# Scores and PV of an attention kernel in one place on TensorE from unit 14 on, with half of PV in two banks of the matmul pool

## Chip, cores and metric

One core of a Trainium2 chip. The metric is the time of one execution in microseconds of device time, given as a median over runs. "Span" is the time from the first to the last instruction in the trace; it is some 1.7 us shorter than the run's time.

## The reference

Attention within chunks of 64 rows, followed by a two-layer network whose activation is h * sigmoid(beta * h).

```python
# attention: q, k, v of 8 batches x 8 heads x 576 rows x 64
scores = scale * np.matmul(q_c, k_c.transpose(0, 1, 2, 4, 3))   # within chunks of 64
attn = np.exp(scores - max) / sum
out = np.matmul(attn, v_c)                                        # "PV"
# network: x of 4608 x 512, w_in 512 x 2048, w_out 2048 x 512
h = x @ w_in
g = h * (1.0 / (1.0 + np.exp(-beta * h)))
result = g @ w_out
```

## The kernel before

The 4608 rows are worked off in 18 units of 256, two units to a block, so 9 blocks. While a block's network runs (16 tiles `hps` of x @ w_in, called m0 to m15 here, and four result tiles `ops` of g @ w_out for the block before), the attention of the next block's two units is slipped in between. `tanh` on ScalarE (ACT) and one multiply on VectorE (DVE) turn an `hps` tile into g.

The accumulators take eight PSUM banks: four in the matmul pool, two for scores, two for PV.

```python
ps_p = ctx.enter_context(tc.tile_pool(name="ps_p", bufs=4, space=bass.MemoryType.PSUM))  # hps, ops
ps_s = ctx.enter_context(tc.tile_pool(name="ps_s", bufs=1, space=bass.MemoryType.PSUM))  # scores: 2 banks
ps_x = ctx.enter_context(tc.tile_pool(name="ps_x", bufs=1, space=bass.MemoryType.PSUM))  # PV: 2 banks
...
def emit_sc(u, split=False, later=False):
    qt, kt = qT.pop(u), kT.pop(u)
    sc = ps_s.tile([128, 2, H, CH], FP32, tag="s", name="sc")
    ...                                  # 32 matmuls of 64x64x64
    nc.scalar.activation(out=et, in_=sc, func=ACTF.Exp, scale=scale)
...
def emit_pv(u, where=("x", "s")):        # first half in the PV banks, second half in the score banks
    et = et_t.pop(u)
    for s in range(2):
        i = 2 * u + s
        if where[s] == "p":              # or in two banks of the matmul pool
            x = [ps_p.tile([128, 4, 128], FP32, tag="p", name=f"y{r}") for r in range(2)]
        else:
            pool = {"x": ps_x, "s": ps_s}[where[s]]
            x = [pool.tile([128, 2, 4, 128], FP32, tag=where[s], name="x")]
        ...                              # 16 matmuls of 64x64x65
...
def emit_norm(u, s):                     # DVE: reciprocal of the sums, multiply; this frees the banks
    ...
# a block: items with a position from 0 to 1, sorted, then emitted
for j in range(3, NB):
    items = [(0.02 + 0.98 * m / KFF, 0, ("m", m)) for m in range(KFF)]
    for t in range(4):
        for hf in range(2):
            items.append((0.98 * (t + 0.5 * hf) / 4, 1, ("t", t, hf)))
    if j + 1 < NB:
        for i in range(2):
            items += att_items(2 * j + 2 + i, 0.03 + 0.43 * i, 0.43)   # scores at 0.03, PV at 0.20, ...
```

So a unit interrupts the big matmuls (128 rows, 128 columns, 512 wide) in two places: once for its scores, once for PV. Each is a group of 32 small matmuls in 64x64 tiles of the array; I call such a group a visit.

The softmax here doesn't subtract the row's maximum and nothing guards it: scores larger than these inputs give would overflow.

## Time and profile before

| what | value | from |
|---|---|---|
| time, median of 3 | 288.98 us (288.93 to 289.1) | runs |
| span | 287.5 us | page |
| TensorE (PE) busy | 281.2 us, 98% | page |
| PE busy from 180 to 240 us | 60.00 of 60.00 | windows |
| DVE, ACT busy | 49%, 51% | page |
| cost of one visit of 32 small matmuls | 0.48 us, eight times in units 14 to 17 | starts of single matmuls |

PE is the bound, without a gap in the stretch that the change touches. How the cost of a visit is read is in the prediction.

### The profile page before, as it was taken

Reading aid. Unit: us, or ns where it says so; the run is one execution under the profiler, and the core shown is the slowest. Engines: PE = TensorE matmul, PEld = TensorE weight load, DVE = VectorE, ACT = ScalarE, POOL = GpSimd, SP = SyncE. Lnnn points to the kernel's source line nnn. Section 1 sums busy time; section 2 is a strip of 40 time slices with the busy share of each in tenths; the row PEclk is TensorE's granted clock in tenths of the full one; section 3 lists DMA queues with packets and bytes.
Section 4 is the critical chain, followed back from the end, with each engine's and each line's share of the span. In section 5 each row is a group of like instructions: output and inputs, shape, how many; then the busy total and the mean of one; then the engine's idle time right before and its main releaser. Section 6 shows DMA issues by size and latency. Waiting matters only on the chain.

```text
span 287.5 us, 6650 instructions
## 1 busy us (share of the span) xinstructions
PE 281.2 (98%) x2779; PEld 136.2 (47%) x2779; DVE 141.4 (49%) x253; ACT 146.7 (51%) x224; POOL 95.7 (33%) x125
## 2 busy tenths in 40 slices
PE   8889999999999999999999999999999999999995
PEld 4464456545544444444444444444444444444444
DVE  2678444776567554534454445444453536333300
ACT  4377218774557545454545454555445544444411
POOL 8743579397172992060907060000000000000000
PEclk9999999999999999999999999999999999999999
DMA  8999999999999999999999999614252212010012
GB/s 197 174 197 206 169 178 209 211 163 173 153 94 182 155 176 179 153 130 159 132 167 134 145 155 142 134 49 110 75 113 73 73 39 73 36 39 36 36 73 75
DMA packets 139997, 37.14 MB, mean 129 GB/s; under 512 B 126912, under 2 KB 135488, under 8 KB 139968
## 3 DMA queue, kind: packets, MB, share of 16 engines
q0 software_dynamic: 99136, 17.83, 79.7%
q1 hardware_dynamic: 40688, 18.83, 30.5%
q8 instruction: 22, 0.36, 0.5%
q14 instruction: 7, 0.06, 0.1%
q10 hardware_dynamic: 144, 0.07, 0.1%
HBM read 36.71 MB, written 9.44 MB: 161 GB/s over the span
## 4 chain that ended last, share of the span: by engine, by line
PE 94%; DMA 3%; ACT 1%; issue 1%; DVE 0%; POOL 0%; DVEq 0%; POOLq 0%
PE hps L322 44%; PE ops L354 42%; DMA h<-in_k_dram 3%; PE x L264 2%; PE sc L236 1%; PE sc L223 1%; PE ops L580 1%; ACT xt L297 1%; PE xp L296 1%; PE sc L196 0%; ACT et L206 0%; POOL h L394 0%; PE warm L374 0%; PE xp L304 0%; DVE xt L297 0%
## 5 line engine op out<-in xcount | busy, mean ns | idle before, releaser
L336 DVE SCALAR_TENSOR_TENSOR gt<-sg,hps 128x512 f16<-128x512 f32 (+1 forms) x153 | 99.1, 654 | 108.5 <-ACT sg L332 108.3
L332 ACT ACTIVATE sg<-hps,beta 128x512 f32<-128x512 f32 (+1 forms) x153 | 100.4, 663 | 74.0 <-PE hps L322 73.9
L322 PE MATMUL hps<-xt,win 128*128 128x512 f16 (+1 forms) x612 | 136.7, 367 | 0.8 <-ACT xt L297 0.7
L354 PE MATMUL ops<-wout,gt 128*128 128x512 f16 x560 | 131.3, 379 | 0.0
L322 PEld LDWEIGHTS <-win 128*128 128x128 f16 x612 | 58.0, 98 | 61.9 <-issue 1.0
L354 PEld LDWEIGHTS <-gt 128*128 128x128 f16 x560 | 53.7, 98 | 63.1
L364 ACT ACTIVATE osb<-ops 128x512 f32<-128x512 f32 x35 | 20.9, 598 | 42.2 <-PE ops L354 42.2
L112 POOL DMA_DIRECT2D vbig<-in_v_dram x40 | 34.0, 872 | 10.3 <-DMA wout<-in_moe_w_out_dram 3.7
L98 POOL DMA_DIRECT2D qu<-in_q_dram x22 | 18.7, 865 | 39.5 <-DMA qT<-qu 37.2
L280 DVE TENSOR_TENSOR x<-x,rd 128x512 f16<-128x512 f32 x34 | 23.5, 692 | 1.3
L98 POOL DMA_DIRECT2D ku<-in_k_dram x22 | 18.9, 880 | 0.1
L278 DVE RECIPROCAL rd<-x 128x8 f32<-128x8 f32 x34 | 6.8, 201 | 11.1 <-PE x L264 11.1
L245 ACT ACTIVATE et<-sc 128x1024 f16<-128x1024 f32 (+1 forms) x8 | 6.4, 811 | 8.2 <-PE sc L236 8.2
L229 ACT ACTIVATE et<-sc 128x1024 f16<-128x1024 f32 x10 | 10.1, 1015 | 0.0
L264 PEld LDWEIGHTS <-et 64*64 64x64 f16 x576 | 6.0, 107 | 7.3 <-issue 3.4
L374 PE MATMUL warm<-idle 128*128 128x512 f16 x24 | 8.6, 515 | 0.0
L264 PE MATMUL x<-vbig,et 64*64 64x65 f16 x544 | 7.8, 195 | 0.2 <-ACT et L206 0.2
L104 POOL DMA_DIRECT2D ku<-in_k_dram x9 | 6.8, 755 | 2.5 <-DMA win<-in_moe_w_in_dram 1.3
L104 POOL DMA_DIRECT2D qu<-in_q_dram x9 | 6.8, 767 | 1.9 <-DMA win<-in_moe_w_in_dram 1.1
L592 DVE TENSOR_SCALAR osb<-ops 128x256 f32<-128x256 f32 (+1 forms) x2 | 0.7, 358 | 12.1 <-PE ops L580 12.1
L130 POOL DMA_DIRECT2D win<-in_moe_w_in_dram x8 | 6.0, 751 | 1.2 <-DMA h<-in_k_dram 0.8
L177 DVE STREAM_TRANSPOSE t<-h 128x512 f32<-128x512 f32 x4 | 4.2, 1084 | 4.2 <-ACT h L176 3.7
(46 smaller groups left out, 69.3 us busy)
## 6 DMA issues: line engine op xcount, KB each, us to landing
out_dram<-osb SPq DMA_DIRECT2D x35, 256.0 KB, 3.4
vbig<-in_v_dram POOLq DMA_DIRECT2D x32, 128.0 KB, 7.6
qu<-in_q_dram POOLq DMA_DIRECT2D x20, 128.0 KB, 5.3
ku<-in_k_dram POOLq DMA_DIRECT2D x20, 128.0 KB, 6.6
win<-in_moe_w_in_dram POOLq DMA_DIRECT2D x8, 256.0 KB, 9.7
wout<-in_moe_w_out_dram POOLq DMA_DIRECT2D x4, 512.0 KB, 12.4
qu<-in_q_dram POOLq DMA_DIRECT2D x3, 256.0 KB, 7.3
ku<-in_k_dram POOLq DMA_DIRECT2D x3, 256.0 KB, 8.9
```

What stands on the lines that cost most here:

```text
L98: nc.gpsimd.dma_start(out=tv[off:off + n, sp], in_=src[b, :, s:s + n, :].rearrange("h p d -> p h d"),)
L104: nc.gpsimd.dma_start(out=t[off // 2:(off + n) // 2], in_=src[b, :, s:s + n, :].rearrange("h (p r) d -> p h r d", r=2),)
L112: nc.gpsimd.dma_start(out=vbig[off:off + n, i, :, 0:D], in_=v[b, :, s:s + n, :].rearrange("h p d -> p h d"),)
L229: nc.scalar.activation(out=et, in_=sc, func=ACTF.Exp, scale=scale)
L264: nc.tensor.matmul(out=(x[0][64 * c:64 * c + 64, r, g, 0:D + 1] if len(x) == 1 else x[r][64 * c:64 * c + 64, g, 0:D + 1]), lhsT=(et[64 * r ...
L280: nc.vector.tensor_tensor(out=o, in0=z[..., 0:D], in1=rd[:, r].to_broadcast(list(o.shape)), op=ALU.mult)
L322: nc.tensor.matmul(out=hps[:, 0:n], lhsT=w_in16[m // 2][:, kk, (m % 2) * 128:(m % 2) * 128 + 128], rhs=xr[:, c0 // CH:(c0 + n) // CH, 2 * ...
L332: nc.scalar.activation(out=sg[:, 0:n], in_=hps[:, 0:n], func=ACTF.Tanh, scale=beta2[:, m:m + 1])
L336: nc.vector.scalar_tensor_tensor(out=gt_t[j][:, m, c0:c0 + n], in0=sg[:, 0:n], scalar=1.0, in1=hps[:, 0:n], op0=ALU.add, op1=ALU.mult,)
L354: nc.tensor.matmul(out=ops, lhsT=gt_t[j][:, kk, t * 128:(t + 1) * 128], rhs=w_out16[kk // 4][:, kk % 4, :], start=(kk == 0), stop=(kk == K ...
L364: nc.scalar.activation(out=osb, in_=ops, func=ACTF.Copy, scale=0.5)
L374: nc.tensor.matmul(out=d[:, 0:w], lhsT=idle[:, 0:128], rhs=idle[:, 0:w])
```

## The change

Its intent: enter the small tiles less often. From unit 14 on, PV of a unit and the scores of the next stand in one place, so units 14 to 17 need five visits, not eight. For this, PV's second half may not lie in the score banks, since the next scores follow at once; it goes, first in order, into two of the four matmul-pool banks. The scores of unit 14 move ahead into block 5, and so do the transposes of unit 15.

```diff
+    MU = 14
@@ emit_pv
-        for s in range(2):
+        for s in (1, 0) if u >= MU else (0, 1):
@@
+    def emit_norms(u):
+        for s in (1, 0) if u >= MU else (0, 1):
+            emit_norm(u, s)
+            emit_xt_dma(u, s)
@@ the items of a block
-            if j + 1 < NB:
+            if 2 * j + 2 < MU:
                 for i in range(2):
                     items += att_items(2 * j + 2 + i, 0.03 + 0.43 * i, 0.43)
+                if 2 * j + 4 == MU:
+                    items += [(0.80, 2, ("sc", MU)), (0.82, 3, ("T", MU + 1))]
+            elif j + 1 < NB:
+                for i in range(2):
+                    items.append((0.15 + 0.5 * i, 2, ("hop", 2 * j + 2 + i)))
@@ emitting them
+                elif it[0] == "hop":
+                    emit_pv(it[1], ("x", "p"))
+                    if it[1] + 1 < NU:
+                        emit_sc(it[1] + 1)
+                    if it[1] + 2 < NU:
+                        emit_T(it[1] + 2)
+                    emit_norms(it[1])
```

In the list of items, `sc` are the scores of a unit, `T` the transposes of its q and k, `norm` the work of DVE that empties the PV banks, and `hop` a merged visit.

## The prediction

> **What bounds the kernel now.** I first read the page's busy times, the clock row and the chain that ended last.
>
> ```profile
> PE 281.2 (98%) x2779; PEld 136.2 (47%) x2779; DVE 141.4 (49%) x253; ACT 146.7 (51%) x224; POOL 95.7 (33%) x125
> PEclk9999999999999999999999999999999999999999
> PE 94%; DMA 3%; ACT 1%; issue 1%; DVE 0%; POOL 0%; DVEq 0%; POOLq 0%
> ```
>
> TensorE (PE) is busy for 98% of the span at full clock, and the chain is 94% PE. DVE and ACT are half idle. Busy can hide gaps, because matmuls overlap, so I asked for the stretch that the change touches:
>
> ```profile
> 180.00:240.00 60.00, 60.00 (x517) 27.45 (x516) 28.68 (x49) 30.91 (x46) 0.00 (x0) 1.00 0.34 81
> ```
>
> 60.00 of 60.00 us are busy on PE (columns: length, then PE, weight load, DVE, ACT, POOL). GpSimd issues nothing more there. So the only thing to gain is PE time spent badly, and any wait that reaches PE is paid in full. The PE timeline shows where time is spent badly:
>
> ```profile
> 196.76 1.89 PE L322 MATMUL hps<-xt,win 128*128 128x512 f16 x8
> 198.58 0.45 PE L223 MATMUL sc<-qT,kT 64*64 64x64 f16 x32
> 198.96 1.90 PE L354 MATMUL ops<-wout,gt 128*128 128x512 f16 x8
> 200.69 1.89 PE L322 MATMUL hps<-xt,win 128*128 128x512 f16 x8
> ```
>
> The columns are start, length, engine, line, and the group. I read starts, not lengths, since one matmul shows 379 ns but eight take 1.73 us, 216 ns each. From 196.76, eight matmuls end their turn at 198.49; scores start at 198.58, 0.09 late. The 32 small matmuls hold PE until 198.96, and the next eight take 1.73, of which the records of single instructions show 10 ns more than usual for the first. By those records a visit costs: entry 93 ns, first to last small start 252, last start to next large start 125, slow first large one 10; 480 together. All eight visits of units 14 to 17 (four of scores, four of PV) read 470 to 472 plus 10. Streaming needs 8 turns of 4 at 32 ns, 256; so some 220 ns of each visit are the price of going in and out. Is that price paid per visit, not per matmul? An earlier visit of 64 small ones answers:
>
> ```profile
> 80.22 2.54 PE L322 MATMUL hps<-xt,win 128*128 128x512 f16 x11
> 82.69 0.71 PE L236 MATMUL sc<-qT,kT 32*64 32x64 f16 x64
> 83.33 1.04 PE L322 MATMUL hps<-xt,win 128*128 128x512 f16 x4
> 84.20 1.89 PE L354 MATMUL ops<-wout,gt 128*128 128x512 f16 x8
> ```
>
> It starts at 82.69, 0.09 after 80.22 + 11 x 0.216, and lasts 0.64; with the 10 ns it costs 0.74 us, not 0.96. So it is paid per visit.
>
> **What the Trainium skill says.** "TensorEngine Tiling (Array Packing)", Key Properties: changing the tiling mode, not just the tile, drains TensorE. The trace agrees: 64*64 groups between 128*128 groups cost 93 ns on entry and a late exit. The change lives on this. "PSUM — Partial Sum Buffer", Terms: there are eight banks of 2 KiB per partition, and two engines may not be in one bank and quadrant at once. The kernel's pools take all eight (4 for the matmul pool, 2 for scores, 2 for PV), so PE must wait until DVE or ACT has finished reading a bank. The trace of before shows these waits as met in time, with no PE idle after 16 us.
>
> **The change part by part.** Per unit, before has two visits, scores and PV. After has, by the order of instructions in the built kernel: scores of 14 alone, earlier, late in block 5; then PV(14)+scores(15), PV(15)+scores(16), PV(16)+scores(17); then PV(17) alone. The matmuls are the same, 5560 PE rows in both. DVE gains 4 rows: each PV half in two banks is normalised in two pieces. These rows lie in idle DVE time, except where they delay a release.
>
> *Gain.* Eight visits become five. A merged visit is 0.74 us (the 64-matmul visit above) against 2 x 0.48 = 0.96: 0.22 saved, three times: **-0.66 us**.
>
> *Wait 1: scores of 14, moved into block 5.* They use the score banks, which still hold the second half of PV(13) there. In after they come behind the matmul tile m12 of block 5. Everything until then has the same order in both kernels, so before's trace gives the times:
>
> ```profile
> 176.80 1.89 PE L354 MATMUL ops<-wout,gt 128*128 128x512 f16 x8
> 176.86 0.69 DVE L336 SCALAR_TENSOR_TENSOR gt<-sg,hps 128x512 f16<-128x512 f32 x1 [2.38 <-ACT sg L332]
> ...
> 178.30 0.68 DVE L336 SCALAR_TENSOR_TENSOR gt<-sg,hps 128x512 f16<-128x512 f32 x1
> 178.53 1.89 PE L322 MATMUL hps<-xt,win 128*128 128x512 f16 x8
> 178.90 0.20 DVE L278 RECIPROCAL rd<-x 128x8 f32<-128x8 f32 x1
> 179.13 0.69 DVE L280 TENSOR_TENSOR x<-x,rd 128x512 f16<-128x512 f32 x1
> ```
>
> m12 is the first half of the group at 178.53. Its turn ends at 179.39, and scores would start at 179.48 with the entry. The multiply that empties PV(13)'s second half ends at 179.13 + 0.69 = 179.82. A release takes about 0.06 to reach PE: early in the kernel a copy ends at 14.98 + 0.58 = 15.56 and the matmul that waits for it starts at 15.62.
>
> ```profile
> 14.98 0.58 ACT L297 COPY xt<-xp 128x512 f16<-128x512 f16 x1 [0.36 <-PE xp L296]
> 15.62 0.27 PE L322 MATMUL hps<-xt,win 128*128 128x256 f16 x1 [0.67 <-ACT xt L297]
> ```
>
> So 179.88 against 179.48: **+0.40 us**, once.
>
> *Wait 2: the matmul pool during a merged visit.* PV's second half takes two of its four banks. In after each merged visit stands between two hps tiles, and the next ops tile follows; by the release order it gets the bank of the hps tile just before the visit. Call that tile's start 0. The chain is read in before's timeline:
>
> ```profile
> 200.69 1.89 PE L322 MATMUL hps<-xt,win 128*128 128x512 f16 x8
> 201.76 0.69 ACT L332 ACTIVATE sg<-hps,beta 128x512 f32<-128x512 f32 x1 [1.47 <-PE hps L322]
> 202.47 0.69 DVE L336 SCALAR_TENSOR_TENSOR gt<-sg,hps 128x512 f16<-128x512 f32 x1 [2.38 <-ACT sg L332]
> ```
>
> Tanh starts 1.07 after the tile, DVE 1.78, and DVE ends at 2.47; with 0.06, PE may write at 2.53. PE wants it after the tile (0.86), the merged visit (0.74) and one more tile (0.87): 2.47. **+0.06, three times: +0.18 us.** After PV(17) there are no scores, so PE wants it 0.26 earlier, at 2.21: **+0.32 us**.
>
> *What I checked and count as zero.* The tile right behind the visit uses the bank of an ops copy that ends at 0.85; it is wanted at 1.60. The PV banks themselves are emptied by about 3.0 and 3.6 (DVE free at 2.38; per bank a reciprocal of 0.17 and a multiply of 0.42, which overlap a little) and are wanted at 4.2 and 5.1. The exponential of the scores (1.0 us) ends at 2.7, when tanh of the next tile becomes ready. The transposed x of units 15 and 17 is issued behind the q and k transposes; in the quiet stretch those take 1.25 us each to issue and x 1.19, landing 2.4 later: about 212 us for unit 15, wanted at about 214.6. q and k of 15 are transposed about 2 us earlier now and land some 3 us before use.
>
> *Sum.* -0.66 + 0.40 + 0.18 + 0.32 = **+0.24 us**. 288.98 + 0.24 = **289.2 us**.
>
> **The rivals.** *A: the gain as intended, no waits*: 288.98 - 0.66 = 288.3. For it: DVE is half idle, and before shows no PE wait here. Against it: the waits before scores of 14 and after PV(17) have margins of -0.4 and -0.3 us by the records, not by guess. *B: the two banks lent to PV starve the matmuls badly*, because the norms stand in DVE's queue before the next tiles' work: each visit loses up to 1 us, so about 291 to 292. For it: two of four banks are gone for some 3 us. Against it: those banks are wanted over 1 us after they come free, and the copies and tanh in between have room. *C: the merge saves less*, since PV uses other rows, banks and weights than scores and the second group's waits for DMAs are queue instructions in the middle of 128 small ones: up to 0.3 us lost per visit. Then 289.5 to 289.8. The 64-matmul visit speaks against it, but it is all of one kind. *D: hidden anyway*: not on this engine, which has no slack.
>
> **Range and chances.** Gain and waits are each under 1 us, against 5.8 us that 2% would take. The gain is sure to about 0.2; the three waits of 0.06 could vanish or double; the three runs of before spread over 0.17. So 288.5 to 289.9, and within 2% at 0.98.
>
> **What would show it.** In after: PE idle before scores of 14 of about 0.4 us, released by the multiply of PV(13); three visits of 64 small matmuls costing 0.74 each; a short idle before the ops tile two tiles on, longest (0.3) after PV(17). It is wrong if PE shows no idle there (A), if merged visits cost 0.9 or more (C), or if tiles of hps wait for the norms of y (B).

## The result, and the profile after

The changed kernel took 289.45 us (median of 6; 289.24 to 290.13), the kernel before 289.13 in the same measurement (median of 6; 288.93 to 289.5). The ratio is 1.0014, with a 95% interval of 1.0001 to 1.0027: within 2%, and if anything slower. Ratios are the mean time of one kernel's fast runs over that of the other's of the same rounds, so not quite the ratio of the medians that I quote.

The page of the changed kernel, its busy times and the chain that ended last:

```profile
PE 279.8 (97%) x2779; PEld 136.2 (47%) x2779; DVE 142.2 (49%) x261; ACT 147.1 (51%) x224; POOL 95.6 (33%) x125
PE 93%; DMA 3%; ACT 1%; issue 1%; DVE 1%; POOL 0%; DVEq 0%; POOLq 0%
```

PE has as many instructions, is 1.4 us less busy, and yet the span is 0.3 us longer: PE now stands still somewhere. Part of that is at the start of the run, where the first loads arrive at slightly different times in every run; in the profiled runs the first `hps` tile started between 15.34 and 16.8 us. So I measure all kernels below over one section of their traces: from the big matmul ahead of the scores of unit 8 (at about 97 us) to the start of the last matmul. It is 186.86 us before and 187.21 after: +0.35 us. This section is my yardstick, because it leaves out the noise of the start, which is larger than nearly every effect here. Each kernel has one trace, but the yardstick repeats well: its first part, up to the tile ahead of PV(13), which no edit touches in ten of the twelve kernels, lasts 76.955 to 76.962 us in all ten.

The windows from 180 to 240 us and from 60 to 180 us (columns: length, then busy us and instructions of PE, weight load, DVE, ACT, POOL; clock; DMA) show where PE stands still:

```profile
180.00:240.00 60.00, 59.85 (x518) 27.88 (x514) 29.26 (x57) 30.89 (x46) 0.00 (x0) 1.00 0.39 81
60.00:180.00 120.00, 119.63 (x1298) 55.93 (x1299) 63.09 (x111) 63.82 (x94) 55.91 (x68) 1.00 1.70 152
```

0.15 us of idle PE in the first, 0.37 in the second, where before had none. The timeline of PE around the scores of 14 and, further down, around PV(17) (start, length, group, and in brackets the idle time ahead of it with what ended it):

```profile
178.48 1.03 PE L328 MATMUL hps<-xt,win 128*128 128x512 f16 x4
179.88 0.45 PE L224 MATMUL sc<-qT,kT 64*64 64x64 f16 x32 [0.37 <-PE hps L328]
...
233.69 1.03 PE L328 MATMUL hps<-xt,win 128*128 128x512 f16 x4
234.65 0.32 PE L265 MATMUL y<-vbig,et 64*64 64x65 f16 x16
234.79 0.30 PE L265 MATMUL x<-vbig,et 64*64 64x65 f16 x16
235.03 1.04 PE L328 MATMUL hps<-xt,win 128*128 128x512 f16 x4
236.22 0.38 PE L360 MATMUL ops<-wout,gt 128*128 128x512 f16 x1 [0.15 <-DVE gt L342]
```

The turn of the tile at 178.48 ends at 179.34 (four times 0.216), and the scores start at 179.88: an entry of 538 ns by the single records, where a normal one is 93. The releaser named, an `hps` matmul, cannot be the cause, since its turn had ended half a microsecond before. The DVE line of the same timeline points to the real one, which two experiments below test:

```profile
179.09 0.69 DVE L286 TENSOR_TENSOR x<-x,rd 128x512 f16<-128x512 f32 x1
```

It ends at 179.78, and PE starts 0.1 later. After PV(17), the `ops` tile at 236.22 should have started at 235.90 (235.03 + 0.87): 0.32 late, behind the DVE multiply that ends at 236.16 (the line below). The bracket says 0.15 only because the last matmul's modelled end lies past its turn; distances between starts do not have this flaw.

```profile
235.47 0.69 DVE L342 SCALAR_TENSOR_TENSOR gt<-sg,hps 128x512 f16<-128x512 f32 x1 [1.90 <-ACT sg L338]
```

The merged visits, PV(15) with scores of 16:

```profile
204.38 1.03 PE L328 MATMUL hps<-xt,win 128*128 128x512 f16 x4
205.33 0.32 PE L265 MATMUL y<-vbig,et 64*64 64x65 f16 x16
205.49 0.29 PE L265 MATMUL x<-vbig,et 64*64 64x65 f16 x16
205.69 0.45 PE L224 MATMUL sc<-qT,kT 64*64 64x64 f16 x32
206.07 1.04 PE L328 MATMUL hps<-xt,win 128*128 128x512 f16 x4
206.94 1.89 PE L360 MATMUL ops<-wout,gt 128*128 128x512 f16 x8
```

The tile's turn ends at 205.24; the next one starts at 206.07 and its first matmul is 10 ns slow: 0.84 us. The three merged visits cost 0.80, 0.84 and 0.84 us. The `ops` tile at 206.94 comes exactly after its `hps` tile: no wait there. The whole difference, from the records of both traces:

| term | predicted, us | in the trace, us |
|---|---|---|
| three merged visits for six | -0.66 | -0.40 (2.48 for 6 x 0.48) |
| scores of 14 wait for their banks | +0.40 | +0.445 |
| `ops` tile behind each of three merged visits | +0.18 | 0 |
| `ops` tile behind PV(17) | +0.32 | +0.316 |
| sum | +0.24 | +0.36; section +0.35 |

### The profile page after: what moved, and what is told of

Read it like the earlier page. It is cut to its first block, busy times and chain, and to the rows that moved or that the text cites. A ratio compares the mean times of both kernels' runs of the same rounds, so it can differ in the third digit from the quotient of the medians.

```text
span 287.8 us, 6657 instructions
## 1 busy us (share of the span) xinstructions
PE 279.8 (97%) x2779; PEld 136.2 (47%) x2779; DVE 142.2 (49%) x261; ACT 147.1 (51%) x224; POOL 95.6 (33%) x125
## 4 chain that ended last, share of the span: by engine, by line
PE 93%; DMA 3%; ACT 1%; issue 1%; DVE 1%; POOL 0%; DVEq 0%; POOLq 0%
PE hps L328 43%; PE ops L360 42%; DMA h<-in_k_dram 3%; PE x L265 2%; PE sc L237 1%; PE sc L224 1%; PE ops L598 1%; ACT xt L303 1%; PE xp L302 1%; PE sc L197 0%; ACT et L207 0%; POOL h L400 0%; PE y L265 0%; ACT sg L338 0%; DVE gt L342 0%
## 5 line engine op out<-in xcount | busy, mean ns | idle before, releaser
L286 DVE TENSOR_TENSOR x<-x,rd 128x512 f16<-128x512 f32 x30 | 20.7, 692 | 1.1
L284 DVE RECIPROCAL rd<-x 128x8 f32<-128x8 f32 x30 | 6.0, 201 | 12.5 <-PE x L265 12.5
L380 PE MATMUL warm<-idle 128*128 128x512 f16 x24 | 7.4, 454 | 0.0
L265 PE MATMUL x<-vbig,et 64*64 64x65 f16 x480 | 7.2, 194 | 0.2 <-ACT et L207 0.2
```

Of the source, the lines that this page charges most:

```text
L265: nc.tensor.matmul(out=(x[0][64 * c:64 * c + 64, r, g, 0:D + 1] if len(x) == 1 else x[r][64 * c:64 * c + 64, g, 0:D + 1]), lhsT=(et[64 * r ...
L286: nc.vector.tensor_tensor(out=o, in0=z[..., 0:D], in1=rd[:, r].to_broadcast(list(o.shape)), op=ALU.mult)
L380: nc.tensor.matmul(out=d[:, 0:w], lhsT=idle[:, 0:128], rhs=idle[:, 0:w])
```

## The experiments

What was open: is the entry to the scores of 14 really the banks; is the gap after PV(17) really the pool; why do merged visits cost more than the 64-matmul visit in the kernel before; and what does the second part of the change, the two banks, buy?

### Scores of 14 one tile later

```diff
-  items += [(0.80, 2, ("sc", MU)), (0.82, 3, ("T", MU + 1))]
+  items += [(0.83, 2, ("sc", MU)), (0.84, 3, ("T", MU + 1))]
```

> The changed kernel with one thing moved: the scores of unit 14 come one matmul tile later in block 5 (behind m13, not m12), so the score banks are free by the time PE gets there. My theory (wait 1: the 0.445 us entry to that visit is PE waiting for DVE to empty the score banks of PV(13)): the entry falls from 538 ns to 93 ns, the visit costs 0.48 us, nothing else changes, and the time falls by 0.44 us against the changed kernel: about 289.0, ratio to before 0.9997. Rival (the early place itself is dear, whatever the banks do, as other work of block 5 is disturbed): the entry stays above 0.3 us or the same time turns up as PE idle elsewhere, ratio stays at 1.001.

Measured: 288.98 us, ratio to before 0.9989 (0.9977 to 1.0001). In the timeline of PE:

```profile
178.25 1.89 PE L328 MATMUL hps<-xt,win 128*128 128x512 f16 x8
180.07 0.45 PE L224 MATMUL sc<-qT,kT 64*64 64x64 f16 x32
180.45 1.90 PE L360 MATMUL ops<-wout,gt 128*128 128x512 f16 x8
```

Entry 0.09 (178.25 + 8 x 0.216 = 179.98), no idle, and nothing else of block 5 was disturbed. The section is 0.49 us shorter than that of the changed kernel, 0.445 of it here and 0.04 by a cheaper merged visit. The theory holds: the early place cost only the wait for DVE.

### PV(17) in the score banks

```diff
-  emit_pv(it[1], ("x", "p"))
+  emit_pv(it[1], ("x", "p" if it[1] + 1 < NU else "s"))
```

> The changed kernel, but the second half of PV(17), after which no scores come, goes into the score banks as in the kernel before, not into two banks of the matmul pool. My theory (the 0.316 us before the ops tile two tiles on comes from the pool being two banks short): that gap is 0, PV(17) costs 0.48 us, and the time falls by 0.32 us against the changed kernel: about 289.1, ratio to before 1.0001. Rival (the gap comes from DVE being late with that tile for another reason): the gap stays.

Measured: 289.4 us, ratio 1.0009 (0.9994 to 1.0025). The profile, on PE, around PV(17):

```profile
234.93 1.03 PE L328 MATMUL hps<-xt,win 128*128 128x512 f16 x4
235.88 0.45 PE L265 MATMUL x<-vbig,et 64*64 64x65 f16 x32
236.26 1.04 PE L328 MATMUL hps<-xt,win 128*128 128x512 f16 x4
237.14 1.67 PE L360 MATMUL ops<-wout,gt 128*128 128x512 f16 x7
```

The `ops` tile follows after 0.88, without a gap. The section is 0.40 us shorter than the changed kernel's: 0.316 of the gap, the rest in merged visits (all three at 0.80 here). The times alone would not have shown it: the profiled run of this kernel took 290.45 us, since its first `hps` tile started 1.2 us later. An effect of 0.3 us is read from a trace, not from six times.

### Both

The two edits above together.

> Both mendings together: scores of 14 one tile later, PV(17)'s second half in the score banks. If the changed kernel's loss is exactly the sum of its terms, what is left are five visits: 0.48 + 0.80 + 0.84 + 0.84 + 0.48 = 3.44 us against eight at 0.48 = 3.85 in the kernel before: 0.41 us less than before, about 288.7, ratio 0.9986. If the two waits only move elsewhere once removed (rival: the bank pressure comes out at another place), the ratio is 0.999 to 1.001 and PE shows idle outside the visits.

Measured: 288.72 us, ratio 0.9978 (0.9966 to 0.999). The section is 186.37 us, 0.49 less than before (0.41 expected; the merged visits were 0.80 in all three). From 180 to 240 us PE is busy throughout again:

```profile
180.00:240.00 60.00, 60.00 (x520) 27.98 (x519) 29.81 (x56) 31.27 (x46) 0.00 (x0) 1.00 0.40 83
```

So the loss of the changed kernel was the two waits (0.76 us; another 0.08 us of the gain over the changed kernel are the cheaper merged visits), and they did not come out at another place. With them gone, the intent of the change is worth 0.2%.

### Touching q and k ahead of the visit

The three merged visits of the changed kernel differ: 0.80, 0.84, 0.84. In each there is one semaphore instruction of 51 ns on PE's queue, ahead of the scores: the scores need two transposes (q and k), which are two DMAs. In the cheap visit it ran 110 ns after the first small matmul, in the dear ones 251 and 257 ns after, just when PV's last matmuls were going. It did not wait for a late DMA: in all three visits both transposes had landed 5 us or more before. This run, on top of both edits, takes it out of the visit.

```diff
 # in emit_m, ahead of the tile before a merged visit (v: the unit whose scores come; the choice of v is cut)
+  nc.tensor.matmul(out=hps[:, 0:1],
+                   lhsT=kT[v].rearrange("p h s e -> p (h s e)")[:, 0:128],
+                   rhs=qT[v].rearrange("p h s e -> p (h s e)")[:, 0:1])
```

> As the run with both mendings, and one tiny 128-wide matmul (1 column, its result overwritten) that reads the transposed q and k of the next unit is put ahead of the matmul tile before each merged visit, so PE has seen both DMAs before the visit starts. My theory for the 60 to 100 ns by which a merged visit is dearer (0.80, 0.84, 0.84 us) than the 0.74 I predicted: a semaphore instruction of 51 ns on PE's queue in the middle of the visit, because scores wait for two DMAs[...]; then the visits fall to 0.74 to 0.75 us with no semaphore instruction in them, while each small matmul costs 0.05 to 0.1 us of its own, so the time moves by less than 0.15 us either way against the run with both mendings. Rival (going from PV's operands to those of scores costs that itself): the visits stay at 0.80 to 0.84 us.

Measured: 288.87 us, ratio 0.9993 (0.9975 to 1.0011). The semaphore instruction is gone from the visits, and all three cost 0.80 us. So the 0.05 to 0.06 above 0.74 are not the semaphore instruction: this part of my theory fell. What the instruction can explain is the step from 0.80 to 0.84, which showed only where it fell late: in two of three visits in the changed kernel, in one in the run with the scores of 14 later. The run with both edits has the instruction too and shows 0.80 three times, but there it ran early each time, 98 to 105 ns after the first small matmul. So late and dear go together in every visit; that the one causes the other is not shown, and what makes it fall late I did not settle. The tiny matmul itself cost 28 ns.

### The early place alone, on the kernel before

```diff
+  if j == 6:
+      items.remove(next(it for it in items if it[2] == ("sc", 14)))
+  if j == 5:
+      items.append((0.80, 2, ("sc", 14)))
```

> One part of the change alone, on the kernel before: only the scores of unit 14 are moved to the early place in block 5, everything else stays, no merged visits. My theory: this part alone costs what it cost in the changed kernel, entry 538 ns instead of 93, so the time rises by 0.44 us to about 289.6 to 289.7 (ratio 1.0015), and the other seven visits stay at 0.48 us. Rival (the wait appears only together with the merged visits or with the earlier transposes of unit 15): entry at most 0.15 us, time unchanged.

Measured: 289.5 us, ratio 1.0006 (0.9989 to 1.0023); too near to 1 to decide anything. The trace decides: the entry is 535 ns, the other seven visits are as before, the section is 0.44 us longer than before's. And here the profile names the cause, a multiply that ends at 179.71 by DVE's own line, 0.10 ahead of the scores:

```profile
178.41 1.03 PE L322 MATMUL hps<-xt,win 128*128 128x512 f16 x4
179.81 0.45 PE L223 MATMUL sc<-qT,kT 64*64 64x64 f16 x32 [0.37 <-DVE x L280]
```

`x L280` is the multiply that empties PV's second half from the score banks. The wait belongs to the place alone, not to the merging.

### Without the two banks

```diff
-  emit_pv(it[1], ("x", "p"))
+  emit_pv(it[1], ("x", "s"))
+  emit_norms(it[1])
   if it[1] + 1 < NU:
       emit_sc(it[1] + 1)
   if it[1] + 2 < NU:
       emit_T(it[1] + 2)
-  emit_norms(it[1])
```

> The changed kernel without its second part: PV's second half goes into the score banks as before, so the scores of the next unit in the same visit must wait until DVE has normalised that half (the norms are issued ahead of the scores). This shows what the two banks of the matmul pool buy. My theory: DVE gets to the norm 2.38 us after the start of the matmul tile before the visit, the reciprocal and multiply take until 3.31, PE may write at 3.37, and wants to at about 1.21, so PE stands still for 2.1 to 2.2 us in each of three visits: about 6 us more than the changed kernel (without its 0.32 after PV(17)), near 295.5, ratio to before 1.021 to 1.023. Rival (the norm could be had in time, so the two banks were not needed): under 1 us more.

Measured: 297.19 us, ratio 1.0282 (1.0251 to 1.0313); 1.7 us more than expected. The timeline of the first merged visit, DVE and PE:

```profile
192.21 0.20 DVE L284 RECIPROCAL rd<-x 128x8 f32<-128x8 f32 x1
192.45 0.69 DVE L286 TENSOR_TENSOR x<-x,rd 128x512 f16<-128x512 f32 x1
...
193.24 0.64 PE L224 MATMUL sc<-qT,kT 64*64 64x64 f16 x32 [2.01 <-issue]
193.81 1.89 PE L328 MATMUL hps<-xt,win 128*128 128x512 f16 x4
195.49 2.22 PE L360 MATMUL ops<-wout,gt 128*128 128x512 f16 x7
```

The wait is as worked out: between PV's last group and the first scores lie 2.22 us, in all three visits. What I had not expected follows it in the first: four `hps` matmuls take 1.68 us from 193.81 to 195.49, not 0.86. Single starts there are 427 ns apart, not 216, until about 196.4, and the clock row shows it:

```profile
PEclk9999999999999999999999999979999999999999
```

After standing still for 2.2 us TensorE ran at half rate for some 3.2 us. This cost about 1.55 us (1.36 in the big matmuls, 0.19 in the visit's own small ones), once in three equal standstills, and is what my expectation lacked. Why only the first was followed by it, the runs do not show. With PV ahead of the scores, the two banks are thus worth some 6.6 us of waits; against that stand 0.3 us after PV(17), and the run with the score banks for PV(17) avoids even these.

### Scores ahead of PV

As with both edits, and the order inside a merged visit turned round.

```diff
-  emit_pv(it[1], ("x", "p" if it[1] + 1 < NU else "s"))
   if it[1] + 1 < NU:
       emit_sc(it[1] + 1)
+  emit_pv(it[1], ("x", "p" if it[1] + 1 < NU else "s"))
```

> As the run with both mendings, but in each merged visit the scores of the next unit come ahead of PV, not behind. There the second DMA wait is at the head of the visit, where PE's queue still holds matmuls of 216 ns. My theory after four runs: a merged visit has a floor of 0.79 + 0.01 us, since 128 instructions in a row outrun what the queue is fed with, and 40 to 45 ns more in visits where the 51 ns semaphore instruction falls late. So here all three visits at 0.79 to 0.80, none at 0.83, and the time equals the run with both mendings within 0.1 us. Rival (the 50 ns of the floor come from scores following PV): 0.74 us each, 0.15 us less in all.

Measured: 288.77 us, ratio 0.9979 (0.9963 to 0.9995). My theory fell, the rival was right about the visits: they cost 0.737 + 0.010, the 0.74 to 0.75 of the prediction, in all three. But the section is only 0.01 us shorter than with both edits, for this reason:

```profile
204.84 0.45 PE L224 MATMUL sc<-qT,kT 64*64 64x64 f16 x32
205.12 0.30 PE L265 MATMUL y<-vbig,et 64*64 64x65 f16 x16
205.25 0.31 PE L265 MATMUL x<-vbig,et 64*64 64x65 f16 x16
205.49 1.04 PE L328 MATMUL hps<-xt,win 128*128 128x512 f16 x4
206.41 1.89 PE L360 MATMUL ops<-wout,gt 128*128 128x512 f16 x8
```

From the `hps` tile to the `ops` tile it is 0.92, not 0.87: 50 to 52 ns in each of the three visits. This is the wait for the bank of the tile before the visit, which the prediction put at 0.06 and which the changed kernel did not show. It was not absent there; the dearer visit had covered it. Faster visits bring it out, and the gain is nil. DVE's line shows the release, at 205.67 + 0.69 = 206.36, 0.05 ahead of the `ops` tile:

```profile
205.67 0.69 DVE L342 SCALAR_TENSOR_TENSOR gt<-sg,hps 128x512 f16<-128x512 f32 x1 [1.90 <-ACT sg L338]
```

### Scores twice

As with both edits, with the 32 score matmuls of a merged visit issued twice to the same place (the result is right).

```diff
-  for jj in range(H):
+  for jj in (range(H) if u <= MU else [n for _ in range(2) for n in range(H)]):
```

> As the run with both mendings, but the 32 score matmuls of each merged visit are issued twice, to the same place with the same result: 96 small matmuls in a visit. This measures what a further small matmul costs in a long visit. Theory of the feed (late in a long visit weight loads start 8 to 9 ns apart, so a matmul with its weight load takes 16 to 17 ns once the queue has run dry): 32 more cost 0.53 us each visit, visits of about 1.32 us, 1.6 us more in all than the run with both mendings, about 290.3. Rival (only the array counts, four matmuls every 32 ns as in short visits): 0.26 us more each, 1.05 us visits, 0.8 us more in all, about 289.5.

Measured: 289.68 us, ratio 1.0008 (0.9987 to 1.0029). A visit of 96 costs 1.09 us, 0.29 more than one of 64; the section is 0.87 us longer for three. In the lines below, the 64 scores and the big tile that follows:

```profile
206.24 0.78 PE L224 MATMUL sc<-qT,kT 64*64 64x64 f16 x64
206.95 1.04 PE L328 MATMUL hps<-xt,win 128*128 128x512 f16 x4
```

So a theory of mine fell once more: a long visit doesn't fall to half the rate. Late in it four small matmuls take 33 to 34 ns in place of 32, no more. The extra 0.05 us in visits with PV ahead is made of single steps of 43 to 58 ns between groups of four, among the scores that follow PV: two in a visit of 64, four in this one. With scores ahead of PV there is none after the first group.

### Merged visits from unit 12, from unit 10

The version with scores first, with `MU = 12` and `MU = 10`, to see whether more of it is better.

> The run with scores first, with merged visits from unit 12 on, not 14: five in place of three. My account per merged visit after eight runs: 0.75 us for the visit plus 0.05 us wait for the bank of the matmul tile before it, against two visits of 0.48: 0.16 us saved. So 0.33 us less than the run with scores first: ratio to before 0.9967 to 0.9970, about 288.4. Rival (q, k and v of the earlier units are not there in time, since GpSimd's loads run until 190 us and the transposes now come half a unit sooner): PE waits for a DMA of over 0.3 us, and the ratio is 0.998 or more.

> The same with merged visits from unit 10 on: seven. By the same account 0.65 us less than the run with three: ratio to before 0.9956 to 0.9960, about 288.1. Rival as before, and likelier here: PE waits for transposes or loads, ratio 0.997 or more.

Measured: 290.03 us, ratio 1.0027 (1.0015 to 1.0039), and 290.62, ratio 1.0061 (1.004 to 1.0083): slower, the rival was right. The waits of PE, its timeline and the landing of transposed q around the first merged visit, with `MU = 12`:

```profile
PE sc L224 <- DMA qT<-qu: 1.7, 1, 1.7
```

```profile
159.72 1.03 PE L328 MATMUL hps<-xt,win 128*128 128x512 f16 x4
162.42 0.44 PE L224 MATMUL sc<-qT,kT 64*64 64x64 f16 x32 [1.67 <-DMA qT<-qu]
```

```profile
DMA to landing us min/median/max: 5.9/8.8/8.8
```

The transpose was issued at 153.46 and took 8.8 us to land, while GpSimd's loads were still moving; in the kernel before, after 180 us, the same takes 3.1: there the last of the loads has landed at 176.6 (not at 190, as the expectation has it). That the loads are the reason is inferred from this, not tested; nor did I try to issue this one transpose earlier. Only the first merged visit waits (entry 1.83 us with 12, 2.57 with 10); the later ones cost 0.75, as they should. The account per visit was right, the price of starting early was not in it. Of the three beginnings tried, unit 14 is the best as the transposes are placed.

## Why the prediction was right

The time was foretold as 289.2, in 288.5 to 289.9, and was 289.45; the effect as +0.24, and was +0.32 by the medians, +0.35 in the section. By its steps:

- **PE has no slack, so a wait is paid in full.** Right: the terms of the trace add up to the section's difference within 0.01 us.
- **The gain, -0.66.** Too large; it was -0.40. This is the step of the prediction that was mis-sized, and the missing waits below follow from it. The step was "a merged visit is 0.74 us", taken from a visit of 64 matmuls of one kind (scores in 32x64 tiles, before unit 8). With scores behind PV a visit costs 0.80 to 0.84. The run with the order turned round has 0.747, so 0.05 is the order (in the run that touches q and k early there is no semaphore instruction in the visits either, and they stay at 0.80); the 0.04 in some visits goes with a semaphore instruction that falls late. Rival C named both of these as risks ("other rows, banks and weights", "queue instructions in the middle"), at up to 0.3 us per visit; it was 0.06 to 0.10.
- **Wait 1, +0.40.** Right in mechanism and nearly in size: 0.445, as the release took 0.10 us to reach PE here and not 0.06. It was removed by moving one item, and made by moving one item in the kernel before.
- **Waits of 0.06 behind each merged visit.** Not in the changed kernel; the chain was right, however, since PE came 0.05 to 0.1 us later than assumed. With visits of the assumed length the wait is 0.05. The two errors are one: what the visit lost, the wait no longer cost, so the sum erred less than its terms. The prediction had not foreseen this; that its sum came so near is in part luck.
- **+0.32 after PV(17).** Right: 0.316, gone with the score banks.
- **What counted as zero** did not show up as PE waits. Rival A (no waits) and B (starved matmuls) did not happen. The prediction counted 4 more instructions on DVE; there are 8 (261 against 253); and q and k of unit 15 landed 5.3 us ahead of their use (185.7 against 191.0), not 3. No PE wait came of either.

Open is why scores behind PV make steps of 43 to 58 ns, and what decides whether the semaphore instruction falls late.

## What to carry to other kernels

On an engine without slack a saving of switches is real, but so is every new wait; look up for each moved group which buffer it needs, who frees it, and when that happened in the old trace, to 0.1 us. Here one group moved by one tile, and other banks for one half of PV(17), turned a loss of 0.1% into a gain of 0.2%. When effects are below half a per cent, measure them between two marks in the trace and not by the run's time, and do not expect two gains to add: a wait hidden behind a slow visit appears when the visit is made fast.

## What the Trainium skill lacked or had wrong

- "TensorEngine Tiling (Array Packing)", Key Properties, says that changing the tiling mode drains TensorE, but gives no price. Here: 93 ns on entry, some 103 on leaving (125 ns from the last small start, where 22 would pass to the next group of four), 20 more for the first group of four, 10 more for the first big matmul: some 0.22 us per visit.
- "TensorE: Matmul & The Clock Gate", Back-to-back issue gap, gives about 131 ns per matmul of 512 columns as the sustained rate with weight loads; this case, a stream of such pairs, shows 216 ns at full clock in every stretch of big matmuls, which is what the section gives for an isolated matmul.
- The same page, its table "Why this matters for your kernels", warns of PE idle gaps above some 3 us. Here a gap of 2.22 us was followed by half rate (427 ns in place of 216) for about 3.2 us, in one of three equal gaps.
- No page that I read has the cost of a semaphore instruction on PE's queue among small matmuls: 51 ns long; visits where it ran about 0.1 us after the first small matmul cost what visits without it cost, those where it ran 0.25 us after cost 0.04 us more.
- No page that I read says that the order of two kinds of small matmuls in one tiling mode matters: PV then scores 0.80 us, scores then PV 0.75.
